# Windowed attention and a two-layer feed-forward: the weights' conversion is untied from the blocks before it, and its low words, loads and row bounds go to other engines

## The chip, the cores and the metric

The kernel runs on one core of a Trainium2 chip. The metric is the device time of one execution in microseconds. Before the change three runs took 990.71, 990.72 and 995.53 us, median 990.72. The engines are TensorE (PE, matmuls and transposes into PSUM), VectorE (DVE), ScalarE (ACT), GpSimd (POOL) and SyncE (SP, which here only starts DMAs). Each takes its instructions in the order in which the program was scheduled.

## The reference

```
scores = q k^T / 8 - slope_h |i - j|,   only 0 <= i - j < 128, else -1e9     # 8 x 8 heads, 576 rows, 64 wide
attn   = softmax(scores);   x = attn v, heads side by side: 4608 x 512
h = x @ w_in                                                               # 512 -> 2048
g = h where h >= 1;  0 where h <= -1;  (h + 1)^2 / 4 between
out = g @ w_out                                                            # 2048 -> 512, 4608 x 512
```

Q, K and V come as 32-bit floats, the weights w_in and w_out as 64-bit floats, which the kernel sees as two 32-bit words a number: a low word and a high word.

## The kernel before, in words

The 4608 rows are worked in 12 chunks of 384. For each chunk come the attention of four pairs of heads (a pair fills the 128 partitions) and then the feed-forward in 16 blocks of 128 hidden units. The program interleaves by hand: the list `segments` holds the steps of attention, the list `ffn` those of the feed-forward, and while the feed-forward of chunk c is emitted, the segments of chunk c + 1 are emitted between its steps (L799 to L807). The marks `ready` say up to which segment a chunk's attention must have been emitted before its feed-forward begins. A scheduler then orders the instructions of each engine by the order of emission and by when it expects an operand to be there; `behind(instructions, f)` (L238) adds edges, so that what f emits stands on its engine behind the given instruction of the same engine.

Attention of a pair: `scores` (L433, matmuls at L443), `soften` (L465: a VectorE operation L482 with bias and row extreme, ScalarE's exponential L484, then L490 to L495 on VectorE), `weights_t` (L499: transposes L504, ScalarE's copy L508, and two selects on GpSimd, L509 and L511, that make the tile `lu`), `values` (L525, matmuls at L538). `reach_of_v` (L380) takes the row maxima of V on VectorE (L385).

A block of the feed-forward: `layer1` (L587: 12 matmuls L590 to L592 of 16-bit high and low parts; then u by ScalarE at L597 and g by VectorE at L598 and L599), and two blocks later `layer2` (L610; in chunk 0 32-bit matmuls at L619, later 16-bit ones at L622 to L624). From chunk 1 on GpSimd makes the low part of g (L607).

The weights are converted once, while attention and feed-forward of chunk 0 run. For each of the 16 blocks:

- `fetch_weights` (L171) starts two DMAs from ScalarE's queue (L173, L175) into one of three buffers of raw words.
- `unfold` (L177): ScalarE maps the high words (L180) and the low words (L181), 128 x 1024 each, in place.
- `float32_of` (L183, VectorE at L185) joins both into a 32-bit float, once for w_in (`f_i`) and once for w_out (`wf`).
- `convert_in` (L189) also takes the row maxima of `f_i` on VectorE (L194); `convert_out` (L216) takes the row sums of |wf| on ScalarE (L219).
- `scale_in` (L197, through `scale_of` at L154): a matmul spreads the row bounds over the partitions (L152), VectorE reduces them (L159) and makes a power of two and its inverse (L161 to L163).
- `split_in` (L204): one more small product (`fall_in`, L202), the 16-bit high part on ScalarE (L210) and the low part on VectorE (L211).

Blocks 0 to 2 are converted during the attention of chunk 0: `convert_early` (L766) puts the two halves of each behind the heads listed in `EARLY` (L761). The others are converted by `convert_after(f)` (L749), emitted after layer 1 of block f for block f + 3, and each step is tied by `behind(done_g[f], ...)` to u and g of that block.

## Time and profile before

| what | value |
|---|---|
| median of three runs | 990.72 us |
| the profiled execution, its own time | 991.8 us |
| its span, first to last instruction | 989.7 us |
| mean granted TensorE clock | 0.989 |
| VectorE busy in the span | 731.6 us (74%) |
| ScalarE busy in the span | 607.2 us (61%) |
| GpSimd busy in the span | 340.6 us (34%) |

The page and the answers of the trace give times in microseconds from the first instruction of the span, and the mean time of one instruction of a group in nanoseconds. A row names the line of the kernel, the engine, the operation, the written and read tiles and their shape. "x16" is a count. The text in brackets, or behind the second bar of a group, is idle time of the engine just before the instruction and what ended it. "ACTq" and "SPq" are the DMA issues of these engines' queues; they are not counted as busy.

### The profile page before, as it was taken

The numbers are of one execution on the slowest core, as the hardware profiler recorded it, in microseconds if no ns is written. First come the engines' busy times: TensorE is split into PE (matmuls) and PEld (weight loads), VectorE is DVE, ScalarE is ACT, GpSimd is POOL, SyncE is SP. The second block draws the span as 40 slices with busy tenths as digits, with TensorE's granted clock in tenths as the row PEclk, the third lists the DMA queues.
The fourth block names the chain that finished last, engine by engine and source line by source line (L and its number), as shares of the span: only waits on it lengthen the run. The fifth ranks groups of instructions, "written<-read, shape, count | busy, mean of one in ns | idle before, by whom it ended". The sixth has DMA issues, their size and how long they took to land.

```text
span 989.7 us, 17764 instructions
## 1 busy us (share of the span) xinstructions
PE 955.0 (96%) x6181; PEld 522.2 (53%) x6181; DVE 731.6 (74%) x2089; ACT 607.2 (61%) x1509; POOL 340.6 (34%) x446
## 2 busy tenths in 40 slices
PE   8798899998999999999999999999999999999997
PEld 5444344554555555555555555555555555555553
DVE  6899798896787787687787788677677886765332
ACT  6788777666656666565665665666666655644322
POOL 5311003333334432532533533433443443334221
PEclk9799999998999999999999999999999999999999
DMA  8476441012021011112111101111201000000000
GB/s 274 134 245 201 154 141 39 12 49 72 30 59 58 25 41 63 38 30 60 62 33 52 58 25 54 63 30 50 72 30 30 33 1 1 33 2 1 33 1 32
DMA packets 53290, 59.86 MB, mean 60 GB/s; under 512 B 3408, under 2 KB 42576, under 8 KB 53200
## 3 DMA queue, kind: packets, MB, share of 16 engines
q1 hardware_dynamic: 42304, 41.82, 13.7%
q10 hardware_dynamic: 10896, 16.91, 4.9%
q8 instruction: 48, 0.79, 0.3%
q14 instruction: 42, 0.34, 0.1%
HBM read 49.28 MB, written 9.44 MB: 59 GB/s over the span
## 4 chain that ended last, share of the span: by engine, by line
PE 85%; DVE 7%; ACT 4%; DMA 1%; issue 1%; POOL 1%; ACTq 0%; SPq 0%; POOLq 0%; DVEq 0%
PE h L590 12%; PE h L592 12%; PE h L591 12%; PE acc L622 12%; PE acc L623 12%; PE acc L624 12%; PE s L459 5%; PE x L561 4%; PE p L504 3%; ACT z L484 1%; PE acc L619 1%; DMA vn<-in_v_dram 1%; DVE g L598 1%; ACT raw L181 1%; DVE g L599 1%
## 5 line engine op out<-in xcount | busy, mean ns | idle before, releaser
L607 POOL TENSOR_TENSOR gl<-g,gh 128x384 f16<-128x384 f32 x176 | 167.2, 950 | 453.5 <-ACT gh L606 442.7
L598 DVE SCALAR_TENSOR_TENSOR g<-u,half 128x384 f32<-128x384 f32 x176 | 123.9, 705 | 157.1 <-ACT u L597 144.1
L606 ACT CAST gh<-g 128x384 f16<-128x384 f32 x176 | 89.6, 509 | 189.2 <-DVE g L599 102.1
L622 PE MATMUL acc<-wo,gh 128*128 128x512 f16 x528 | 200.3, 379 | 0.0
L623 PE MATMUL acc<-wo,gh 128*128 128x512 f16 x528 | 200.2, 379 | 0.0
L624 PE MATMUL acc<-wo,gl 128*128 128x512 f16 x528 | 196.0, 379 | 0.0
L597 ACT ACTIVATE u<-h,shift,fall 128x384 f32<-128x384 f32 x176 | 116.4, 663 | 98.9 <-PE h L592 98.9
L484 ACT ACTIVATE z<-z,nmax 128x256 f32<-128x256 f32 (+2 forms) x288 | 137.7, 480 | 33.1 <-DVE nmax L482 31.1
L590 PE MATMUL h<-x,wi 128*128 128x384 f16 x384 | 125.8, 329 | 4.6 <-ACT x L570 2.8
L590 PE MATMUL h<-xh,wi 128*128 128x384 f16 x384 | 125.2, 327 | 4.3 <-ACT wi L210 2.9
L592 PE MATMUL h<-xh,wi 128*128 128x384 f16 x384 | 125.3, 326 | 1.1 <-DVE wi L211 1.1
L592 PE MATMUL h<-x,wi 128*128 128x384 f16 x384 | 126.1, 328 | 0.0
L591 PE MATMUL h<-x,wi 128*128 128x384 f16 x384 | 126.0, 328 | 0.0
L591 PE MATMUL h<-xl,wi 128*128 128x384 f16 x384 | 125.4, 327 | 0.0
L482 DVE CUSTOM_DVE_ANT_0 z<-s,near,z_of 128x256 f32<-128x256 f32 (+2 forms) x240 | 98.6, 459 | 33.7 <-PE s L459 33.5
L599 DVE SCALAR_TENSOR_TENSOR g<-h,gain,g 128x384 f32<-128x384 f32 x176 | 108.1, 615 | 3.9
L590 PEld LDWEIGHTS <-wi 128*128 128x128 f16 x768 | 75.2, 98 | 67.1 <-issue 7.5
L591 PEld LDWEIGHTS <-wi 128*128 128x128 f16 x768 | 75.4, 98 | 59.1 <-issue 7.2
L592 PEld LDWEIGHTS <-wi 128*128 128x128 f16 x768 | 75.3, 98 | 53.9 <-issue 3.6
L519 POOL TENSOR_SCALAR_AFFINE_SELECT lu<-lu 128x768 f16<-128x768 f16 x80 | 70.4, 894 | 58.2 <-DVE lu L517 57.7
L624 PEld LDWEIGHTS <-gl 128*128 128x128 f16 x528 | 51.5, 98 | 59.0 <-issue 0.4
L622 PEld LDWEIGHTS <-gh 128*128 128x128 f16 x528 | 51.6, 98 | 51.0 <-issue 1.1
(148 smaller groups left out, 1445.7 us busy)
## 6 DMA issues: line engine op xcount, KB each, us to landing
out_dram<-o SPq DMA_DIRECT2D x35, 256.0 KB, 2.1
raw<-in_moe_w_in_dram ACTq DMA_DIRECT2D x16, 512.0 KB, 4.6
raw<-in_moe_w_out_dram ACTq DMA_DIRECT2D x16, 512.0 KB, 5.5
vn<-in_v_dram SPq DMA_DIRECT2D x32, 256.0 KB, 2.8
qk<-in_q_dram SPq DMA_DIRECT2D x40, 192.0 KB, 2.4
qk<-in_k_dram SPq DMA_DIRECT2D x28, 256.0 KB, 2.8
vn<-in_v_dram SPq DMA_DIRECT2D x16, 192.0 KB, 2.6
qk<-in_k_dram SPq DMA_DIRECT2D x12, 192.0 KB, 2.5
```

The lines of the kernel that those rows point to most:

```text
L482: a = V.tensor_tensor_reduce(out=z[:, i, c0:], in0=pt[:, n, c0:], in1=r[:, c0:], op0=ALU.add, op1=ALU.min, scale=factor, scalar=3.0e38, ac ...
L484: b = S.activation(z[:, i, c0:], z[:, i, c0:], AF.Exp, bias=nmax[:, i:i + 1], scale=-1.0, accum_out=sm[:, i, 0:1])
L590: T.matmul(ph, wi[fc][:, 0, cc, :], xh, start=(cc == 0), stop=False)
L591: T.matmul(ph, wi[fc][:, 0, cc, :], xl, start=False, stop=False)
L592: T.matmul(ph, wi[fc][:, 1, cc, :], xh, start=False, stop=(cc == NCC - 1))
L597: first = S.activation(u, ph, AF.Relu, bias=shift[c] if c else quarter, scale=fall[c][:, col])
L598: V.scalar_tensor_tensor(g, u, half[c] if c else 0.5, u, ALU.min, ALU.mult)
L599: last = V.scalar_tensor_tensor(g, ph, gain[c][:, col] if c else fall[c][:, col], g, ALU.mult, ALU.max)
L607: G.tensor_tensor(gl, g, gh, ALU.subtract)
L622: T.matmul(a, gh[:, ts], wo[fc][:, 0], start=first, stop=False)
L623: T.matmul(a, gh[:, ts], wo[fc][:, 1], start=False, stop=False)
L624: T.matmul(a, gl[:, ts], wo[fc][:, 0], start=False, stop=last)
```

## The change

Seven edits, in the order of the diff:

1. The loads of the weights are started by SyncE; those of blocks 1 and 2 follow a small memset on GpSimd. That of block 0 is put behind the first two pairs' loads of Q and K.
2. The low words are mapped by GpSimd.
3. The row bounds of w_in are sums of absolute values by ScalarE instead of maxima by VectorE. Blocks 0 and 1 keep a column each; from block 2 on two blocks share a tile of two columns.
4. `scale_in` works on all columns of such a tile at once, so it is called for every second block; `fall_in` moves into it.
5. Around pair 4 (the first of chunk 1), the values of pairs 2 and 3 and the transposes of pair 3 are emitted ahead of the scores of pair 4, and the mark `ready` with them.
6. The maxima of V of pairs 4 to 7 are all emitted in step 4 instead of steps 3 and 4.
7. The ties to `done_g` go from `convert_after` and from `split_in`; `EARLY` is one head earlier in its last two entries.

```diff
     def fetch_weights(fc):
         w = raw[fc] = rawp.tile([P, 2, DM, 2], I32, name=f"raw{fc}", tag=f"raw{fc % 3}")
-        S.dma_start(w[:, 0].rearrange("p (c f) w -> p c f w", c=NCC),
-                    wi32[:, 2 * fc * P:2 * (fc + 1) * P].rearrange("(c p) (f w) -> p c f w", p=P, w=2))
-        S.dma_start(w[:, 1], wo32[fc * P:(fc + 1) * P, :].rearrange("p (f w) -> p f w", w=2))
+        if 0 < fc < 3:
+            G.memset(w[:1, :, 0, :1], 0)
+        DMA.dma_start(w[:, 0].rearrange("p (c f) w -> p c f w", c=NCC),
+                      wi32[:, 2 * fc * P:2 * (fc + 1) * P].rearrange("(c p) (f w) -> p c f w", p=P, w=2))
+        DMA.dma_start(w[:, 1], wo32[fc * P:(fc + 1) * P, :].rearrange("p (f w) -> p f w", w=2))
...
-        S.activation(low, low.bitcast(U32), AF.Copy, scale=0.9375 * 2.0 ** -29)
+        G.tensor_scalar(low, low.bitcast(U32), 0.9375 * 2.0 ** -29, None, ALU.mult)
...
         float32_of(fc, 0, f)
-        rows = column(f"rows_i{fc}", "rows")
-        V.tensor_reduce(rows, f, X, ALU.max, apply_absolute_value=True)
-        spread(f"i{fc}", rows)
+        if fc < 2 or fc % 2 == 0:
+            width = 1 if fc < 2 else 2
+            rows_i[fc] = column(f"rows_i{fc}_{width}", f"rows{width}", n=width)
+        S.activation(junk, f, AF.Abs, accum_out=rows_i[fc] if fc < 2 else rows_i[fc - fc % 2][:, fc % 2:fc % 2 + 1])
 
     def scale_in(fc):
-        s1, i1 = s_in[:, fc:fc + 1], i_in[:, fc:fc + 1]
-        scale_of(f"i{fc}", s1, i1)
+        rows = rows_i.pop(fc)
+        n = rows.shape[1]
+        s1, i1 = s_in[:, fc:fc + n], i_in[:, fc:fc + n]
+        b = bank(f"m_i{fc}")[:, :n * P]
+        across(b, rows)
+        top = column(f"top_i{fc}", f"top{n}", n=n)
+        V.tensor_reduce(top, b.rearrange("p (a w) -> p a w", w=P), X, ALU.max)
+        ti = top.bitcast(I32)
+        V.tensor_scalar(ti, ti, 0x7F800000, None, ALU.bitwise_and)
+        V.tensor_scalar(i1, top, 2.0 ** -100, 1.0 / TOP, ALU.max, ALU.mult)
+        V.reciprocal(s1, i1)
+        if fc > 1:
+            fall_in(fc, n)
...
     for p in range(p8):
+        if p == NPAIR:
+            segments.append([lambda p=p: values(p - 2)])
+            turn(2 * p - 2)
+            turn(2 * p - 1)
+            segments.append([lambda p=p: values(p - 1)])
+            ready.append(len(segments))
         segments += [[lambda p=p: scores(p, (0, 1))], [lambda p=p: scores(p, (2,))]]
...
-            segments += [[lambda d=d, x=x: behind(done_t[d], lambda: reach_of(x))] for x in {3: (4, 5), 4: (6, 7), 6: (8,), 7: (9,)}.get(p, ())]
+            segments += [[lambda d=d, x=x: behind(done_t[d], lambda: reach_of(x))] for x in {4: (4, 5, 6, 7), 6: (8,), 7: (9,)}.get(p, ())]
...
         if c == 0 and fc + 2 < NFC:
-            ops.append(lambda fc=fc: behind(done_g[fc], lambda: split_in(fc + 2)))
+            ops.append(lambda fc=fc: split_in(fc + 2))
...
             if fc + 2 < NFC:
-                behind(done_g[f], lambda: fetch_weights(fc + 2))
-            behind(done_g[f], lambda: convert_in(fc))
-            behind(done_g[f - 1 if f else f], lambda: convert_out(fc))
-        if f + 2 < NFC:
-            behind(done_g[f], lambda: scale_in(f + 2))
+                fetch_weights(fc + 2)
+            convert_in(fc)
+            convert_out(fc)
+        if f + 2 < NFC and f % 2 == 0:
+            scale_in(f + 2)
...
-    EARLY = (2, 3, 4, 5, 7, 8)
+    EARLY = (2, 3, 4, 5, 6, 7)
...
     load_first(1)
+    fetch_weights(0)
     load_v(0)
...
-    landed = S.copy(loaded, pair[0]["qr"][:, :1])
-    behind([landed.ins], lambda: fetch_weights(0))
```

More of the change, by code (lines that the diff above doesn't have):

```diff
@@ L180, in unfold @@
         S.activation(high.bitcast(F32), high.bitcast(F32), AF.Prelu, scale=2.0 ** -112, alpha=2.0 ** 32)
-        S.activation(low, low.bitcast(U32), AF.Copy, scale=0.9375 * 2.0 ** -29)
+        G.tensor_scalar(low, low.bitcast(U32), 0.9375 * 2.0 ** -29, None, ALU.mult)
     def float32_of(fc, a, out):
         V.scalar_tensor_tensor(out.bitcast(I32), raw[fc][:, a, :, 1], 3, raw[fc][:, a, :, 0], ALU.logical_shift_left, ALU.bitwise_or)
-    wide = {}
+    wide, rows_i = {}, {}
     def convert_in(fc):
@@ L192, in convert_in, with fall_in @@
         float32_of(fc, 0, f)
-        rows = column(f"rows_i{fc}", "rows")
-        V.tensor_reduce(rows, f, X, ALU.max, apply_absolute_value=True)
-        spread(f"i{fc}", rows)
+        if fc < 2 or fc % 2 == 0:
+            width = 1 if fc < 2 else 2
+            rows_i[fc] = column(f"rows_i{fc}_{width}", f"rows{width}", n=width)
+        S.activation(junk, f, AF.Abs, accum_out=rows_i[fc] if fc < 2 else rows_i[fc - fc % 2][:, fc % 2:fc % 2 + 1])
     def scale_in(fc):
-        s1, i1 = s_in[:, fc:fc + 1], i_in[:, fc:fc + 1]
-        scale_of(f"i{fc}", s1, i1)
-    def fall_in(fc):
-        V.tensor_scalar(fall[0][:, fc:fc + 1], i_in[:, fc:fc + 1], i_x[0], 0.25, ALU.mult, ALU.mult)
+        rows = rows_i.pop(fc)
[11 more added lines that the diff above has]
+            fall_in(fc, n)
+    def fall_in(fc, n=1):
+        V.tensor_scalar(fall[0][:, fc:fc + n], i_in[:, fc:fc + n], i_x[0], 0.25, ALU.mult, ALU.mult)
     def split_in(fc):
-        if fc > 1:
-            fall_in(fc)
         f, s1 = wide.pop(fc), s_in[:, fc:fc + 1]
@@ L662, in windowed_attention_then_ffn @@
             segments.append([lambda: scale_x(1)])
-        if 2 <= p <= NPAIR:
+        if 2 <= p < NPAIR:
             segments.append([lambda p=p: values(p - 2)])
-        if 1 <= p <= NPAIR:
+        if 1 <= p < NPAIR:
             turn(2 * p - 2)
@@ L668, in windowed_attention_then_ffn @@
         if p >= NPAIR:
-            segments.append([lambda p=p: values(p - 1)])
-            if p == NPAIR:
-                ready.append(len(segments))
+            if p > NPAIR:
+                segments.append([lambda p=p: values(p - 1)])
             turn(2 * p)
```

## The prediction

> **What bounds the kernel now.** I read the page first, then a table of the busy times by stage, then what stopped TensorE inside the slow stages.
>
> ```profile
> PE 955.0 (96%) x6181; PEld 522.2 (53%) x6181; DVE 731.6 (74%) x2089; ACT 607.2 (61%) x1509; POOL 340.6 (34%) x446
> ```
> ```profile
> 20.00:44.00 24.00, 16.16 (x77) 8.87 (x78) 22.91 (x82) 20.09 (x51) 8.18 (x17) 0.79 0.61 194
> 44.00:160.00 116.00, 103.39 (x497) 52.31 (x496) 100.39 (x312) 92.76 (x193) 11.04 (x31) 0.99 0.50 167
> ...
> 225.00:245.00 20.00, 15.56 (x109) 8.25 (x108) 12.85 (x39) 12.34 (x32) 9.10 (x11) 0.83 0.23 76
> 245.00:989.00 744.00, 736.49 (x4953) 403.77 (x4951) 524.85 (x1454) 428.51 (x1090) 275.98 (x323) 1.00 0.12 37
> ```
>
> The columns after the length are busy PE, PEld, DVE, ACT, POOL, then the granted TensorE clock. The kernel is bound by TensorE, but not everywhere: from 245 us on it idles 7.5 of 744 us, while it idles 7.8 of the 24 us from 20 to 44 (attention of row chunk 0) and 12.6 of the 116 us from 44 to 160 (feed-forward of chunk 0, with the conversion of the weights). VectorE is busy 22.91 of 24 there, then 100.39 of 116. So the first 160 us are bound by VectorE's queue, and the change, which works only there, can win at most those 20.4 us and some slow clock. The last rows of the argument are the waits of TensorE and VectorE themselves:
>
> ```profile
> 24.70 0.52 PE L504 MATMUL p<-ident,ep 128*128 128x128 f32 x3 [2.51 <-DVE rc L491]
> 40.27 1.11 PE L538 MATMUL x<-lu,vn 128*64 128x256 f32 x2 [2.85 <-POOL lu L511]
> 69.12 2.84 PE L619 MATMUL acc<-wf,g 128*128 128x512 f32 x6
> 110.48 4.17 PE L619 MATMUL acc<-wf,g 128*128 128x512 f32 x6 [3.07 <-DVE g L599]
> ```
> ```profile
> 22.50 0.69 DVE L385 TENSOR_REDUCE rows<-vn 128x1 f32<-128x512 f32 x1 [0.73 <-DMA vn<-in_v_dram]
> 23.34 0.69 DVE L385 TENSOR_REDUCE rows<-vn 128x1 f32<-128x512 f32 x1
> ```
> ```profile
> DVE g L598 <- ACT u L597: 6.7, 2, 3.7
> ```
>
> The bracket is the idle time before a row and who ended it. TensorE's 2.51 us at 24.70 end with a softmax step that stands behind two reductions of V (L385) on VectorE, the first of which had waited 0.73 us for its load. The 3.07 us before 110.48 end with VectorE's g.
>
> **The change part by part.** *VectorE loses work.* Sixteen maxima of the rows (L194) go, and the powers of blocks 2 to 15 come in seven pairs. This view has all of VectorE's groups between 17 and 157 us that the sum needs (busy us, mean ns):
>
> ```profile
> L211 DVE SCALAR_TENSOR_TENSOR wi<-f_i,s_in,wi 128x512 f16<-128x512 f32 x16 | 12.2, 763 | 1.7 <-ACT wi L210 1.7
> L185 DVE SCALAR_TENSOR_TENSOR wf<-raw 128x512 int32<-128x512 int32 x16 | 11.6, 723 | 0.0
> L185 DVE SCALAR_TENSOR_TENSOR f_i<-raw 128x512 int32<-128x512 int32 x16 | 11.0, 688 | 2.2 <-ACT raw L181 2.2
> L194 DVE TENSOR_REDUCE rows_i<-f_i 128x1 f32<-128x512 f32 x16 | 10.8, 678 | 0.0
> ...
> L598 DVE SCALAR_TENSOR_TENSOR g<-u 128x384 f32<-128x384 f32 x16 | 8.8, 551 | 6.9 <-ACT u L597 6.7
> L495 DVE TENSOR_TENSOR ep<-z,rc 128x384 f32<-128x384 f32 x14 | 7.9, 589 | 0.0
> L494 DVE TENSOR_TENSOR z<-z 128x384 f32<-128x384 f32 (+1 forms) x14 | 7.6, 546 | 0.0
> ...
> L159 DVE TENSOR_REDUCE top_i<-m_i 128x1 f32<-128x128 f32 x16 | 4.5, 282 | 0.2 <-PE m_i L152 0.2
> ...
> L202 DVE TENSOR_SCALAR fall<-i_in,i_x 128x1 f32<-128x1 f32 x16 | 3.1, 194 | 0.0
> ...
> L163 DVE RECIPROCAL s_in<-i_in 128x1 f32<-128x1 f32 x16 | 2.5, 157 | 0.3
> ...
> L162 DVE TENSOR_SCALAR i_in<-top_i 128x1 f32<-128x1 f32 x16 | 2.4, 149 | 0.2
> L161 DVE TENSOR_SCALAR top_i<-top_i 128x1 int32<-128x1 int32 x16 | 2.4, 148 | 0.1
> ...
> L344 DVE TENSOR_REDUCE i<-m 128x2 f32<-128x256 f32 x1 | 0.4, 414 | 0.0
> ```
> ```profile
> 27.10 0.67 DVE L194 TENSOR_REDUCE rows_i<-f_i 128x1 f32<-128x512 f32 x1
> 27.69 0.27 DVE L482 CUSTOM_DVE_ANT_0 z<-s,rel 128x128 f32<-128x128 f32 x1
> ```
>
> From start to start an L194 takes 0.59 us, its tail of 0.09 lies under the next one: 16 x 0.59 = 9.4 us. A pair saves the four small ones, 0.148 + 0.149 + 0.157 + 0.194 = 0.65, and a reduction of one column for the longer one of two (L344 has that shape), 2 x 0.282 - 0.414 = 0.15; 0.80 less five tails of 0.09 is 0.35, and seven times that 2.4 us. Together -11.8 us.
>
> *ScalarE* loses 16 low words (L181) and gains 16 sums of the form of L219.
>
> ```profile
> 27.22 1.14 ACT L181 ACTIVATE raw<-raw 128x1024 int32<-128x1024 uint32 x1
> 28.25 0.62 ACT L219 ACTIVATE junk<-wf 128x512 bf16<-128x512 f32 x1
> 28.77 0.20 ACT L219 ACTIVATION_READ_ACCUMULATOR junk<-wf 128x1 f32 x1
> 28.86 0.47 ACT L544 COPY xn<-x 128x384 f32<-128x384 f32 x1
> ```
>
> That is 16 x (0.61 - 1.03) = -6.7 us. ScalarE is not the fuller queue (92.76 of 116), so this counts nothing in the sum; it is the cover under which the u of a block comes no later. Its 32 DMA issues go too, also counted at nothing, because its busy rows run on beside them.
>
> *GpSimd gains 16 low words of 128x1024.* No such instruction is in the trace. From below, its selects move 384 columns in 0.52 us, 1.4 us for 1024. From above, its own TENSOR_SCALAR:
>
> ```profile
> L127 POOL TENSOR_SCALAR rel<-rel x6: 847/847/1092, 4.4 to 9.0; 128x256 f32<-128x256 f32 x6
> ```
> ```profile
> L511 POOL TENSOR_SCALAR_AFFINE_SELECT lu<-lu 128x384 f32<-128x384 f32 x14 | 8.6, 611 | 0.8
> L509 POOL TENSOR_SCALAR_AFFINE_SELECT lu<-lu 128x384 f32<-128x384 f32 x14 | 8.5, 612 | 52.6 <-ACT lu L508 52.6
> ```
>
> Four times 847 ns is 3.4 us, four times 1092 is 4.4. I take 3.4, the same operation: 54 us, 0.39 of the 140 us. GpSimd had 17.1 us of selects there, so it has room. The Trainium skill ("GPSIMD Engine Reference", section 7) gives about 1.9 cycles an element where the step is at most 8 bytes, as here: at its 1.2 GHz that is, as an estimate, 1.6 us. L127, with a step of 4 bytes, took 4.0 cycles an element, and the measurement decides; with the page's figure the two costs below would be halved and the sum about 4 us better.
>
> *What GpSimd's work costs VectorE.* An operation with two inputs in SBUF is slower beside GpSimd:
>
> ```profile
> L598 DVE SCALAR_TENSOR_TENSOR g<-u,half 128x384 f32<-128x384 f32 x176 | 123.9, 705 | 157.1 <-ACT u L597 144.1
> ```
> ```profile
> 28.66 0.41 DVE L494 TENSOR_TENSOR z<-z 128x256 f32<-128x256 f32 x1
> 32.06 0.66 DVE L494 TENSOR_TENSOR z<-z 128x256 f32<-128x256 f32 x1
> ```
> ```profile
> 31.73 0.72 POOL L511 TENSOR_SCALAR_AFFINE_SELECT lu<-lu 128x384 f32<-128x384 f32 x1
> ```
>
> L598 takes 551 ns in chunk 0, where GpSimd is mostly idle, and 705 later, beside gl: 1.28 times. L494 beside a select took 0.66 instead of 0.41: 1.6 times. The two-input groups above (L211, L185 twice, L598, L495, L494) sum to 59.1 us; 0.39 of them meets a low word. That is +6.4 us at 1.28, +13.8 at 1.6, and nothing from below, if they fall beside other work. I take 1.28, which is a mean over 176, not one case.
>
> *The order around pair 4.* The maxima of V of pairs 4 and 5 leave the place at 22.5: the waits of 0.73 and 0.15 there (0.9 us) go; the reductions themselves are only moved. Chunk 0's last values now come ahead of the scores of pair 4, so that pair 4's softmax fills the 3.7 us in which VectorE waited for the first u; TensorE keeps those scores for the time of the selects. -4.6 us together; from below 0.9, if the fill fails. What is late next is the selects of head 7: block 2 is converted one head earlier (EARLY 6 instead of 7), and its low word can stand on GpSimd between the selects of heads 6 and 7.
>
> *The clock.* The six L619 at 110.48 took 4.17 us instead of 2.84 after the 3.07 us gap. With 0.6 us less of L194 per block ahead of that g, and the reductions of V elsewhere, I count the gap as shortened enough for this to go: -1.4.
>
> *Waits that come.* The selects stand in GpSimd's queue, and the values matmul stands behind them. A select that comes at random finds a low word in 0.39 of the cases and waits half of 3.4: 0.66 us, 14 heads, 9.3 us. TensorE's own waits for them so far (us in total, times, longest):
>
> ```profile
> PE x L538 <- POOL lu L511: 4.1, 3, 2.9
> ```
>
> It waited three times, for seven pairs, and a pair stands behind the later of its two heads: 3/7 x 9.3 / 2 = +2.0. From above: 3.4 for each of seven pairs, 23.8.
>
> *The loads* now stand in SP's queue, in order with those of Q, K and V:
>
> ```profile
> 25.29 7.59 SPq L377 DMA_DIRECT2D vn<-in_v_dram  x2
> ```
>
> Two loads of V held that queue 7.6 us until their small memset on GpSimd had run. Weights behind such a pair are late by as much, but are fetched two blocks, some 14 us, ahead (116 us for 16 blocks is 7 a block): 0, and up to one such wait (7.6) if that lead is gone. The two new memsets hold loads 1 and 2 behind the selects of a head, in the attention of chunk 0, long before their blocks multiply: 0 as well. *The ties taken out* let the scheduler put conversions ahead of u and g. I count them at 0; they bring or cost what the rivals say.
>
> **The sum.** -11.8 + 6.4 - 4.6 - 1.4 + 2.0 = -9.4 us. The profiled run took 991.8 (span 989.7 and 2.1 around it), so 982.4; the median of the runs shown, 990.72, lies 1.1 below the profiled one, so 981.3.
>
> **The rivals.** *Nothing gained:* the overlap costs VectorE 1.6 times, 13.8 us, and the order around pair 4 brings only the 0.9. -11.8 + 13.8 - 0.9 - 1.4 + 2.0 = +1.7, which gives 992.4. For it: VectorE is the full queue, and every conversion puts its low word beside its own two-input steps. Against: 176 rows of L598 say 1.28. The Trainium skill (same page, section 1) names contention with VectorE instructions of two SBUF inputs; the trace agrees, 705 against 551 ns. That the ties bind nothing, since three buffers of raw words set the order anyway, leads to no new case: the sum counts them at 0.
>
> *Slower:* GpSimd becomes the wait. In order, a low word of 3.4 us ahead of a pair's last select delays its values matmul by that much, and TensorE, also in order, stands. The gain without the +2.0 is 11.4 us, so it decides from four pairs of seven on (13.6); five give 17.0 - 11.4 = +5.6, 996.3, all seven +12.4, 1003.1. For it: TensorE already waited 2.85 us for L511 with GpSimd nearly empty. Against: 61% of GpSimd's time is still free of low words, and the scheduler has other blocks to put between.
>
> *More gained:* the conversions run ahead into gaps, and the overlap costs nothing on the path: -11.8 - 4.6 - 1.4 = -17.8, 972.9. For it: 20.4 us of idle TensorE are there to fill. Against: ScalarE and VectorE have little slack in which to run ahead.
>
> **How the numbers follow.** The forecast (976 to 987) has 0.48, more gained (968 to 976) 0.14, nothing gained (987 to 995) 0.20, slower 0.18. The range 970 to 998 leaves out the lower half of "more" and the upper half of "slower", about 0.16. A measurement can tell about 0.5%, 5 us (two runs shown agree to 0.01 us, the third is 4.8 off): faster is below 985.8. Of the forecast some 0.41 of its 0.48 lies there; with 0.14 that is 0.55. Same: 0.07 + 0.20 = 0.27. Slower 0.18. The forecast's own range is 976 to 987.
>
> **What would show it.** Right: no L194; low words on GpSimd of about 3.4 us; L385 of pairs 4 and 5 later than the first h; TensorE's idle time from 20 to 160 us down from 20.4 to about 12; L185 and L211 some 10% longer (0.39 of 1.28); the span after 245 us unchanged. Wrong: low words near 1.5 us (more gained), or L185 waiting for GpSimd instead of ScalarE, or TensorE's waits for lu above 10 us (slower).

## The result, and the profile after

The changed kernel is slower. Five runs of it took 998.07 to 1000.71 us, median 999.65; five of the kernel before, on the same chip, 990.71 to 995.53, median 992.63. The ratio is 1.0067, with a 95% interval of 1.0050 to 1.0084, so about 6.7 us more where 9.4 less was forecast. The profiled execution took 999.68 us, its span is 997.7, its mean granted clock 0.982 (before 991.8, 989.7 and 0.989). The head of the page, after:

```profile
PE 956.7 (96%) x6181; PEld 523.3 (52%) x6181; DVE 726.5 (73%) x2038; ACT 602.8 (60%) x1524; POOL 390.6 (39%) x464
```

VectorE has 5.1 us less to do than before, ScalarE 4.4 less, GpSimd 50 more. None of these sums tells why the kernel is slower. Lines of the changed kernel stand a little lower than those of before: the low word is L183, the join L187 (was L185), the sum of w_in L198, the low part of w_in L223 (L211), the maxima of V L397 (L385), softmax's last step L507 (L495), its transposes L516 (L504), the selects L521 and L523 (L509, L511), the values L550 (L538), layer 1 L602 to L604 (L590 to L592).

The table by stage cuts the early part at 70 us. First before, then after (busy PE, PEld, DVE, ACT, POOL, then the clock):

```profile
20.00:70.00 50.00, 39.98 (x196) 21.68 (x197) 44.46 (x147) 41.95 (x93) 13.33 (x32) 0.90 0.58 187
70.00:160.00 90.00, 79.57 (x377) 39.50 (x376) 78.84 (x247) 70.89 (x150) 5.89 (x16) 0.98 0.49 162
160.00:990.00 830.00, 817.06 (x5497) 447.65 (x5495) 595.31 (x1636) 483.63 (x1227) 310.62 (x359) 1.00 0.12 37
```
```profile
20.00:70.00 50.00, 24.87 (x117) 13.20 (x115) 39.59 (x105) 36.96 (x86) 37.29 (x27) 0.71 0.61 204
70.00:160.00 90.00, 86.31 (x404) 43.90 (x403) 69.82 (x207) 59.40 (x140) 30.00 (x37) 0.97 0.45 147
160.00:998.00 838.00, 827.90 (x5558) 453.26 (x5556) 604.35 (x1669) 495.93 (x1260) 312.72 (x360) 1.00 0.12 37
```

TensorE's idle time in each stretch is its length less its busy time (the last one ends with the span, at 989.7 and 997.7). From 20 to 70 us it went from 10.0 to 25.1, from 70 to 160 from 10.4 down to 3.7, after 160 from 12.6 to 9.8. So TensorE idles 6.7 us less from 70 to 160 us, in the feed-forward of chunk 0, and 15.1 us more in the attention of chunk 0 and the first steps after it. The stretches are cut by the clock, not by the work: the last second-layer matmuls of chunk 0 start at 152.65 us before and at 166.34 after. Beside that, TensorE's busy time rose by 1.7, and its idle time before 20 us by 0.8: 15.1 - 6.7 - 2.8 + 1.7 + 0.8 = 8.1, the span's 8.0. In the same 140 us VectorE is busy 109.4 instead of 123.3, but 9.0 of these 13.9 us only come later: after 160 us it is busy 604.35 instead of 595.31.

The longest waits of TensorE there are these five (timeline of after; start, length, and in brackets the idle time before and who ended it):

```profile
38.01 0.29 PE L152 MATMUL m_i<-ident,rows_i 128*128 128x128 bf16 x1 [4.25 <-ACT junk L198]
41.32 1.12 PE L550 MATMUL x<-lu,vn 128*64 128x256 f32 x2 [2.38 <-POOL lu L523]
45.84 0.29 PE L152 MATMUL m_i<-ident,rows_i 128*128 128x128 bf16 x1 [3.40 <-ACT junk L198]
49.81 2.39 PE L550 MATMUL x<-lu,vn 128*64 128x256 f32 x10 [1.25 <-POOL lu L523]
67.80 1.54 PE L516 MATMUL p<-ident,ep 128*128 128x128 f32 x6 [6.93 <-DVE ep L507]
```

To see why the values stood so late, GpSimd's timeline at that place:

```profile
36.69 2.89 POOL L183 TENSOR_SCALAR raw<-raw 128x1024 int32<-128x1024 uint32 x1 [4.25 <-DMA raw<-in_moe_w_out_dram]
39.64 1.04 POOL L521 TENSOR_SCALAR_AFFINE_SELECT lu<-lu 128x384 f32<-128x384 f32 x1
40.75 0.52 POOL L523 TENSOR_SCALAR_AFFINE_SELECT lu<-lu 128x384 f32<-128x384 f32 x1
41.35 2.89 POOL L183 TENSOR_SCALAR raw<-raw 128x1024 int32<-128x1024 uint32 x1
44.32 1.04 POOL L521 TENSOR_SCALAR_AFFINE_SELECT lu<-lu 128x384 f32<-128x384 f32 x1
45.44 3.21 POOL L183 TENSOR_SCALAR raw<-raw 128x1024 int32<-128x1024 uint32 x1
48.72 1.04 POOL L523 TENSOR_SCALAR_AFFINE_SELECT lu<-lu 128x384 f32<-128x384 f32 x1
```

Head 6's and head 7's selects stand behind three low words, one of them between head 7's own two selects. The first low word itself stood 4.25 us for its load, and everything behind it stood too: ScalarE's copy for head 6, which its selects need, was done by 33.34 (first row below). The last select ends at 49.76. TensorE's two waits for m_i come from conversions as well. The matmul that spreads a block's row bound stands in TensorE's queue ahead of the attention still to do, and the bound is late; ScalarE and VectorE, after:

```profile
32.88 0.46 ACT L520 COPY lu<-p 128x384 f32<-128x384 f32 x1
...
36.24 1.10 ACT L182 ACTIVATE raw<-raw 128x1024 f32<-128x1024 f32 x1 [1.37 <-DMA raw<-in_moe_w_out_dram]
37.25 0.61 ACT L198 ACTIVATE junk<-f_i 128x512 bf16<-128x512 f32 x1
...
45.07 0.63 ACT L198 ACTIVATE junk<-f_i 128x512 bf16<-128x512 f32 x1 [2.64 <-DVE f_i L187]
```
```profile
44.28 0.69 DVE L187 SCALAR_TENSOR_TENSOR f_i<-raw 128x512 int32<-128x512 int32 x1 [1.07 <-POOL raw L183]
```

The sum at 37.25 stood behind a high word (L182) that waited for a load as well, so the first of the two waits comes from a load and not from a low word; the sum at 45.07 stood behind a join that waited for the low word of 41.35. At 67.80 TensorE's queue holds the transposes of pair 4 ahead of the next block's first layer. They wait for VectorE, whose rows there are:

```profile
62.20 2.45 DVE L397 TENSOR_REDUCE rows<-vn 128x1 f32<-128x512 f32 x4
64.57 0.22 DVE L503 RECIPROCAL rc<-rc 128x3 f32<-128x3 f32 x2
64.72 0.99 DVE L610 SCALAR_TENSOR_TENSOR g<-u 128x384 f32<-128x384 f32 x2
65.63 1.58 DVE L187 SCALAR_TENSOR_TENSOR wf<-raw 128x512 int32<-128x512 int32 x1
67.14 0.14 DVE L400 TENSOR_REDUCE rows<-rows 128x1 f32<-128x4 f32 x1
67.20 1.01 DVE L507 TENSOR_TENSOR ep<-z,rc 128x384 f32<-128x384 f32 x2
```

The four maxima of V of pairs 4 to 7, 2.45 us (edit 6 brought two of them here), and a join of 1.58 stand ahead of pair 4's last softmax step.

### The profile page after: what moved, and what is told of

It is laid out like the page before. It is cut to its first block, busy times and chain, and to the rows that moved or that the text cites. A ratio compares the mean times of both kernels' runs of the same rounds, so it can differ in the third digit from the quotient of the medians.

```text
span 997.7 us, 17790 instructions
## 1 busy us (share of the span) xinstructions
PE 956.7 (96%) x6181; PEld 523.3 (52%) x6181; DVE 726.5 (73%) x2038; ACT 602.8 (60%) x1524; POOL 390.6 (39%) x464
## 4 chain that ended last, share of the span: by engine, by line
PE 87%; DVE 4%; DMA 3%; POOL 2%; ACT 2%; issue 1%; SPq 0%; POOLq 0%; ACTq 0%; DVEq 0%
PE h L602 12%; PE h L604 12%; PE h L603 12%; PE acc L634 12%; PE acc L635 11%; PE acc L636 11%; PE s L471 5%; PE x L573 4%; DMA raw<-in_moe_w_out_dram 3%; PE p L516 3%; PE acc L631 2%; POOL raw L183 1%; PE s L455 1%; DMA qk<-in_q_dram 1%; ACT z L496 1%
## 5 line engine op out<-in xcount | busy, mean ns | idle before, releaser
L602 PE MATMUL h<-xh,wi 128*128 128x384 f16 x384 | 125.6, 329 | 3.4 <-DVE g L611 2.3
L602 PE MATMUL h<-x,wi 128*128 128x384 f16 x384 | 125.2, 327 | 3.0 <-DVE g L611 2.7
L604 PE MATMUL h<-x,wi 128*128 128x384 f16 x384 | 125.3, 326 | 0.0
L604 PE MATMUL h<-xh,wi 128*128 128x384 f16 x384 | 125.3, 328 | 0.0
L602 PEld LDWEIGHTS <-wi 128*128 128x128 f16 x768 | 75.2, 98 | 64.0 <-issue 7.9
L604 PEld LDWEIGHTS <-wi 128*128 128x128 f16 x768 | 75.3, 98 | 55.1 <-issue 6.7
```

The lines of the kernel that those rows point to most:

```text
L602: T.matmul(ph, wi[fc][:, 0, cc, :], xh, start=(cc == 0), stop=False)
L604: T.matmul(ph, wi[fc][:, 1, cc, :], xh, start=False, stop=(cc == NCC - 1))
```

## The experiments

Three theories at the start. *Line:* low words, each of them 3 us, stand on GpSimd ahead of the selects of heads 6 and 7, and that is the loss. *Ties:* conversions that run ahead on ScalarE and VectorE are the loss. *Order:* the scores of pair 4, now behind the values of pair 3, leave TensorE without work while it waits, and its clock falls. Each run below stands beside runs of the kernel before on its own chip, median 992.4 to 993.3 us, so a thousandth of a ratio is 1 us. In brackets stands the 95% interval. The diffs show the lines that tell an edit; `...` stands for lines left out.

### The line of GpSimd

**Conversions of blocks 2 to 4 held behind head 7**, all else as after:

```diff
-            convert_in(fc)
-            convert_out(fc)
+            behind(done_t[7] if fc < 5 else [], lambda: (convert_in(fc), convert_out(fc)))
...
-    EARLY = (2, 3, 4, 5, 6, 7)
+    EARLY = (2, 3, 4, 5, 7, 7)
```

> The changed kernel with one thing more: the conversions of blocks 2, 3 and 4 stand behind the selects of head 7 on GpSimd (and behind head 7's steps on the other engines); the low words stay on GpSimd and the ties stay out. Line: head 7's selects end before 43 us, 984 to 992 us. Ties: later blocks still run ahead, 996 to 1000. Order: 996 to 1000.

990.62 us, ratio 0.9974 (0.9958 to 0.9989), 9 us below the kernel after. GpSimd's timeline has the low words behind the last select, which now ends at 37.19 instead of 49.76:

```profile
35.92 0.68 POOL L521 TENSOR_SCALAR_AFFINE_SELECT lu<-lu 128x384 f32<-128x384 f32 x1 [0.64 <-ACT lu L520]
36.67 0.52 POOL L523 TENSOR_SCALAR_AFFINE_SELECT lu<-lu 128x384 f32<-128x384 f32 x1
37.27 9.47 POOL L183 TENSOR_SCALAR raw<-raw 128x1024 int32<-128x1024 uint32 x3
```

The time lies in the range of the line theory and outside those of the other two, and more than the whole loss against before is gone. `done_t[7]` holds instructions of VectorE, ScalarE and GpSimd, though, so the conversions stand behind head 7 on all three engines.

**The ties of edit 7 put back**, EARLY as after:

```diff
-            ops.append(lambda fc=fc: split_in(fc + 2))
+            ops.append(lambda fc=fc: behind(done_g[fc], lambda: split_in(fc + 2)))
...
-                fetch_weights(fc + 2)
-            convert_in(fc)
-            convert_out(fc)
+                behind(done_g[f], lambda: fetch_weights(fc + 2))
+            behind(done_g[f], lambda: convert_in(fc))
+            behind(done_g[f - 1 if f else f], lambda: convert_out(fc))
...
-            scale_in(f + 2)
+            behind(done_g[f], lambda: scale_in(f + 2))
```

> The changed kernel with the ties of the conversion to u and g put back (edit 7 without EARLY). Three theories. Line: on GpSimd the low words of blocks 2 to 4 stand among the selects of heads 6 and 7, so that these end at 49.8 us instead of 41.6; the ties name only instructions of ScalarE and VectorE, so they never bound the low words on GpSimd and putting them back frees nothing there: 995 to 1003 us. Ties: the conversions that ran ahead on ScalarE and VectorE are the cost: 982 to 990. Order: the scores of pair 4, now behind the values of pair 3, leave TensorE without work while it waits, and the clock falls to half: 996 to 1002.

998.79 us, ratio 1.0063 (1.0042 to 1.0083): no better than after. The ties are edges on ScalarE and VectorE, whose instructions `done_g` holds, and hold nothing on GpSimd: two low words, at 34.63 and 40.11, still stand ahead of the last selects there.

```profile
40.11 2.87 POOL L183 TENSOR_SCALAR raw<-raw 128x1024 int32<-128x1024 uint32 x1
43.05 1.04 POOL L523 TENSOR_SCALAR_AFFINE_SELECT lu<-lu 128x384 f32<-128x384 f32 x1
```

The theory of the ties had 982 to 990 and fails as the cause by itself. The last select does end earlier, at 44.09, and from 20 to 70 us TensorE idles 15.7 us instead of after's 25.1; but from 70 to 160 it idles 9.8 instead of 3.7, and the kernel is no faster. It has edits 3 and 4 beside the ties, a company that costs the kernel before 12.8 us (below); that this eats up the earlier start is argued, not shown.

**Low words back on ScalarE**, all else as after:

```diff
-        G.tensor_scalar(low, low.bitcast(U32), 0.9375 * 2.0 ** -29, None, ALU.mult)
+        S.activation(low, low.bitcast(U32), AF.Copy, scale=0.9375 * 2.0 ** -29)
```

> The changed kernel with the low words back on ScalarE, all else as changed. Line: nothing stands among the selects, head 7's end before 42 us, 982 to 991 us. Ties: conversions run ahead on ScalarE with 1 us more each, as slow as the changed kernel or slower, 998 to 1006. Order: TensorE still has no scores in the gap, but the gap is short: 993 to 999.

993.85 us, ratio 1.0006 (0.9992 to 1.0020): 6 us below after, but above the 982 to 991 of the line theory. TensorE still waits for head 7's last select:

```profile
42.39 2.40 PE L550 MATMUL x<-lu,vn 128*64 128x256 f32 x10 [5.76 <-POOL lu L523]
```

Here ScalarE is late: from 35.48 to 39.68 us it maps the high and low words of two blocks, and its copy for head 7 comes behind them, at 40.69.

**Low words back on ScalarE and the conversions held** (both edits):

```diff
-        G.tensor_scalar(low, low.bitcast(U32), 0.9375 * 2.0 ** -29, None, ALU.mult)
+        S.activation(low, low.bitcast(U32), AF.Copy, scale=0.9375 * 2.0 ** -29)
...
-            convert_in(fc)
-            convert_out(fc)
+            behind(done_t[7] if fc < 5 else [], lambda: (convert_in(fc), convert_out(fc)))
...
-    EARLY = (2, 3, 4, 5, 6, 7)
+    EARLY = (2, 3, 4, 5, 7, 7)
```

> The changed kernel with blocks 2 to 4 behind head 7 and the low words back on ScalarE, so that none of GpSimd's costs is left. If the prediction's gains were sized rightly, -11.8 - 4.6 - 1.4 = -17.8 and 973 to 978 us. If they were not, and only GpSimd's queue was harmful, as fast as the changed kernel with the same hold, 987 to 993. If ScalarE's longer conversions take its place, 993 to 998.

994.21 us, ratio 1.0023 (1.0010 to 1.0036). None of GpSimd's costs is left here, and the prediction's gains are not there either: they would have given 973 to 978. With low words on ScalarE holding gains nothing (1.7 us slower, with overlapping intervals), with low words on GpSimd it gains 9.3. What holding mends is there only with the low words on GpSimd. How much of it TensorE feels through the selects, through the row bounds or through the load, these runs don't part.

**The kernel before with low words on GpSimd**:

```diff
-        S.activation(low, low.bitcast(U32), AF.Copy, scale=0.9375 * 2.0 ** -29)
+        G.tensor_scalar(low, low.bitcast(U32), 0.9375 * 2.0 ** -29, None, ALU.mult)
```

> The kernel before with only the low words moved to GpSimd. Line: the low word of block 3 stands ahead of head 6's selects although the ties are in place, since they do not name GpSimd; values of pair 3 some 5 us late, 993 to 999 us. Ties and order: as before, 988 to 993.

994.11 us, ratio 1.0018 (1.0002 to 1.0034). This is in the range of the line theory (993 to 999). Here, with EARLY one head later and the other edits absent, only one low word stands ahead of the last two heads; it ends at 37.20, and the next select waits for ScalarE's copy until 40.85. Edit 2 costs 1.8 us instead of 6.

### The VectorE term

**The kernel before with edits 3 and 4**, ties in place:

```diff
-        V.tensor_reduce(rows, f, X, ALU.max, apply_absolute_value=True)
+        S.activation(junk, f, AF.Abs, accum_out=rows_i[fc] if fc < 2 else rows_i[fc - fc % 2][:, fc % 2:fc % 2 + 1])
...
-        if f + 2 < NFC:
+        if f + 2 < NFC and f % 2 == 0:
             behind(done_g[f], lambda: scale_in(f + 2))
```

> The kernel before with only the row bounds as ScalarE's sums and the powers in pairs (edits 3 and 4), ties kept. The prediction's term was -11.8 us of VectorE, all of it on the path: 979 to 984 us. Rival: the two queues take turns, and 16 sums of 0.61 us on ScalarE take back most of it, 988 to 994. Second rival: the pairs make a scale wait for the next block's conversion, 995 to 1000.

1005.34 us, ratio 1.0129 (1.0114 to 1.0144). This is the term of -11.8 by itself, and it came out at +12.8, beyond even the slowest of the three ranges. Stage and TensorE's waits from 60 us on:

```profile
44.00:160.00 116.00, 94.64 (x443) 47.04 (x440) 84.61 (x244) 95.47 (x204) 10.61 (x29) 0.99 0.48 160
```
```profile
PE acc L629 <- DVE g L609: 6.7, 9, 1.5
PE h L600 <- DVE g L609: 4.8, 1, 4.8
PE h L600 <- ACT wi L220: 3.3, 4, 1.5
```

VectorE is busy 84.61 us instead of 100.39 (718.8 instead of 731.6 in the whole span), so its work did go; but TensorE is busy 8.8 us less as well. From 60 us on it waits for g 11.5 us in these rows, where the kernel before has 3.9; its wait for the high parts of the weights (3.3 us) is about what it was (2.9). Two new theories: *queue*, ScalarE's sums stand ahead of u; *pair*, the power of an even block waits for the conversion of the odd one, which comes a step later.

**The sums alone** (edit 3, single powers):

```diff
-        V.tensor_reduce(rows, f, X, ALU.max, apply_absolute_value=True)
+        S.activation(junk, f, AF.Abs, accum_out=rows)
```

> The kernel before with one line changed: the row bounds of w_in are sums by ScalarE (edit 3) instead of maxima by VectorE; powers stay single (edit 4 left out), ties stay. Edits 3 and 4 together took 12.5 us more than the kernel before. Theory queue (ScalarE is the queue that u stands in, so 16 sums of 0.61 us, 9.8 us, stand ahead of a u): ratio about 1.008 to 1.011, and TensorE's waits for u and h grow as they did with both edits. Theory pair (only the scale that waits for a second block costs): about 0.992 to 0.998, since VectorE loses 9.4 us and ScalarE had 23 of 116 us idle.

989.84 us, ratio 0.9972 (0.9961 to 0.9983).

**The pairs alone** (edit 4, maxima by VectorE):

```diff
-        V.tensor_reduce(rows, f, X, ALU.max, apply_absolute_value=True)
+        V.tensor_reduce(rows_i[fc] if fc < 2 else rows_i[fc - fc % 2][:, fc % 2:fc % 2 + 1], f, X, ALU.max, apply_absolute_value=True)
...
-        if f + 2 < NFC:
+        if f + 2 < NFC and f % 2 == 0:
             behind(done_g[f], lambda: scale_in(f + 2))
```

> The kernel before with the powers of two blocks at once (edit 4) while the row bounds stay maxima by VectorE; ties stay. Theory queue: the pairs save VectorE 2.4 us, ratio 0.997 to 1.000. Theory pair: the scale of an even block stands behind the conversion of the odd one, which comes with the next step, so the first layer of every second block waits for its weights; 12.5 us and a little more, since VectorE keeps its maxima: 1.010 to 1.02, with waits of the first layer's weight loads for the 16-bit weights.

994.53 us, ratio 1.0019 (1.0006 to 1.0032). The sums alone fit the theory of the pair, the pairs alone fit neither: -2.8 and +1.9 alone, +12.8 together. The two cost in company.

**Both, and the ties taken out**:

```diff
...
-            ops.append(lambda fc=fc: behind(done_g[fc], lambda: split_in(fc + 2)))
+            ops.append(lambda fc=fc: split_in(fc + 2))
...
-                behind(done_g[f], lambda: fetch_weights(fc + 2))
-            behind(done_g[f], lambda: convert_in(fc))
-            behind(done_g[f - 1 if f else f], lambda: convert_out(fc))
-        if f + 2 < NFC:
-            behind(done_g[f], lambda: scale_in(f + 2))
+                fetch_weights(fc + 2)
+            convert_in(fc)
+            convert_out(fc)
+        if f + 2 < NFC and f % 2 == 0:
+            scale_in(f + 2)
```

> The kernel before with edits 3 and 4 (sums by ScalarE, powers of two blocks) and, unlike the run that had these two with the ties, with the ties of the conversion taken out too; EARLY, low words, loads and order as before. The sums alone took 2.8 us off, the pairs alone added 1.9, both with the ties added 12.5, and undoing both in the kernel after changed 0.9. Theory tie: the two cost only where the conversion of the next block may not run ahead, so without ties the 12.5 us go: ratio 0.996 to 1.000. Theory queue: sums and pairs together cost in any order as long as the conversion is not crowded out by something else: 1.008 to 1.013.

991.98 us, ratio 0.9989 (0.9973 to 1.0005). The stage from 44 to 160 us, to be held against the row above:

```profile
44.00:160.00 116.00, 105.13 (x511) 54.97 (x509) 92.51 (x267) 99.49 (x221) 13.25 (x33) 0.98 0.51 168
```

ScalarE is fuller than in that run, 99.49 us, and TensorE busy 10.5 us more: the 12.8 need the ties, and a full queue of ScalarE doesn't explain them. With the ties, a pair's second sum may stand on ScalarE only behind a block's u, and the pair's power only behind that sum; that this is the way by which the ties cost is argued, the run shows only that they do.

**The kernel after with edits 3 and 4 undone**:

```diff
-        S.activation(junk, f, AF.Abs, accum_out=rows_i[fc] if fc < 2 else rows_i[fc - fc % 2][:, fc % 2:fc % 2 + 1])
+        V.tensor_reduce(rows, f, X, ALU.max, apply_absolute_value=True)
...
-        if f + 2 < NFC and f % 2 == 0:
+        if f + 2 < NFC:
             scale_in(f + 2)
```

> The kernel after with edits 3 and 4 undone: maxima by VectorE, single powers; low words, loads, order and untied conversion as after. If the 12.5 us that edits 3 and 4 cost the kernel before are in the kernel after as well: ratio to before about 0.994 (987 us). If what binds the kernel after is only the line at heads 6 and 7 (holding the conversions there gave 9.0 us): 1.004 to 1.008, as after.

1000.52 us, ratio 1.0070 (1.0051 to 1.0090), against 1.0067 for after: edits 3 and 4 neither help nor cost there.

**The same with the conversions held** (this diff and that of the first experiment):

```diff
-        S.activation(junk, f, AF.Abs, accum_out=rows_i[fc] if fc < 2 else rows_i[fc - fc % 2][:, fc % 2:fc % 2 + 1])
+        V.tensor_reduce(rows, f, X, ALU.max, apply_absolute_value=True)
...
+            behind(done_t[7] if fc < 5 else [], lambda: (convert_in(fc), convert_out(fc)))
```

> The kernel after with edits 3 and 4 undone and the conversions of blocks 2 to 4 held behind head 7. Holding alone gave 990.6, ratio 0.997. If the cost of the sums and pairs and the cost of the line at heads 6 and 7 are two separate terms: 990.6 less 12.5, 978 us, ratio 0.985, faster than every kernel so far. If they are the same time seen twice: 0.994 to 0.998, no better than holding alone.

991.90 us, ratio 0.9991 (0.9981 to 1.0000), against 0.9974 with the conversions held and edits 3 and 4 in. The 978 us of two separate costs did not come. So in the untied kernel edits 3 and 4 are worth 0.3 us without the hold and 1.7 with it, neither clear of the intervals, and holding gains 7.9 us here too. Of this run and the one before it, from 20 to 70 us:

```profile
20.00:70.00 50.00, 30.40 (x129) 15.78 (x128) 43.34 (x109) 31.37 (x71) 36.19 (x27) 0.69 0.54 183
```
```profile
20.00:70.00 50.00, 37.60 (x162) 19.81 (x161) 44.66 (x119) 33.25 (x76) 37.74 (x32) 0.73 0.54 180
```

The first is without holding, the second with it: VectorE and GpSimd have nearly the same work in both, and TensorE 7.2 us more. Not how full the queues are decides, but the order in them.

The end of head 7's last select on GpSimd goes along with the time, but only roughly. The kernel before, where it ends at 41.60 us, and the runs in which it ends by 43.8 (held with low words on either engine or without edits 3 and 4, low words on ScalarE, low words on GpSimd in the kernel before) took 990.6 to 994.2; the three in which it ends at 44.09 (ties back), 45.55 (edits 3 and 4 undone) and 49.76 (after) took 998.8 to 1000.5. Within each group the order is not kept.

### The order around pair 4

**Edit 5 alone, in the kernel before**:

```diff
+        if p == NPAIR:
+            segments.append([lambda p=p: values(p - 2)])
+            turn(2 * p - 2)
+            turn(2 * p - 1)
+            segments.append([lambda p=p: values(p - 1)])
+            ready.append(len(segments))
         segments += [[lambda p=p: scores(p, (0, 1))], [lambda p=p: scores(p, (2,))]]
```

> The kernel before with only the order around pair 4 (edit 5). The prediction's term was -3.7 for the filled wait for the first u: 986 to 990 us. Rival: TensorE loses the scores of pair 4 as work to do while it waits for the selects of head 7, and the clock stays low longer, 993 to 998.

988.40 us, ratio 0.9958 (0.9941 to 0.9975): -4.2, where the prediction had 3.7 for the fill. The wait that was to be filled did go: from 17 to 157 us VectorE stands 2.9 us for u, at most 1.1 at a time, where the kernel before has 6.7 and 3.7.

**Edit 6 alone, in the kernel before**:

```diff
... (within one line)
-{3: (4, 5), 4: (6, 7), 6: (8,), 7: (9,)}
+{4: (4, 5, 6, 7), 6: (8,), 7: (9,)}
```

> The kernel before with edit 6 alone: the maxima of V of pairs 4 to 7 all in step 4. The prediction counted the two waits of 0.73 and 0.15 us as gone: 0.9 us, ratio 0.999. If the four reductions in one place hold up the softmax of chunk 1 instead, up to 4 x 0.7 us, 1.001 to 1.003.

986.85 us, ratio 0.9943 (0.9929 to 0.9957): -5.7, where 0.9 was counted, and outside both ranges. The fastest of all the kernels tried. TensorE idles 15.0 us from 20 to 160 us instead of 20.4; of the three waits that the prediction showed, 2.51 us at 24.70, 2.85 at 40.27 and 3.07 at 110.48, none is left above 1 us at its place; the longest new one is 2.14, at 36.19.

**Edits 5 and 6 together** (both diffs):

```diff
+            segments.append([lambda p=p: values(p - 1)])
+            ready.append(len(segments))
         segments += [[lambda p=p: scores(p, (0, 1))], [lambda p=p: scores(p, (2,))]]
...
-{3: (4, 5), 4: (6, 7), 6: (8,), 7: (9,)}
+{4: (4, 5, 6, 7), 6: (8,), 7: (9,)}
```

> The kernel before with edits 5 and 6 together: the order around pair 4 and the maxima of V of pairs 4 to 7 in step 4. This is the prediction's term of -4.6 us by itself. Alone the order gave -4.2 us and the maxima -5.7. If they win different idle time: ratio 0.990 (983 us). If they win the same one, 0.9935 to 0.996, as each alone.

994.66 us, ratio 1.0019 (1.0009 to 1.0029): the two gains together are a loss, which neither forecast had. VectorE with edit 6 alone, then VectorE and TensorE with both:

```profile
38.44 2.45 DVE L385 TENSOR_REDUCE rows<-vn 128x1 f32<-128x512 f32 x4
```
```profile
44.32 1.27 DVE L385 TENSOR_REDUCE rows<-vn 128x1 f32<-128x512 f32 x2
45.51 0.17 DVE L491 RECIPROCAL rc<-rc 128x3 f32<-128x3 f32 x1
45.59 1.25 DVE L385 TENSOR_REDUCE rows<-vn 128x1 f32<-128x512 f32 x2
46.75 0.17 DVE L491 RECIPROCAL rc<-rc 128x3 f32<-128x3 f32 x1
46.84 0.59 DVE L584 SCALAR_TENSOR_TENSOR xl<-xn,s_x,xh 128x384 f16<-128x384 f32 x1
```
```profile
47.48 0.48 PE L591 MATMUL h<-xl,wi 128*128 128x384 f16 x1 [2.86 <-DVE xl L584]
```

Alone, edit 6 puts the four maxima at 38.44, before the first layer of chunk 0. With the order of edit 5 they come at 44.32, after that layer has begun, directly ahead of the xl that it waits for, and TensorE stands 2.86 us. That is about half of the 6.1 us by which this run is behind edit 5 alone; the waits for the row bounds of the weights (m_i) grow too, from 1.3 to 5.1 us up to 160. In the kernel after they come at 62.20, ahead of pair 4's softmax, with the wait of 6.93 us behind them.

**Edit 5 with the conversion untied**:

```diff
+            segments.append([lambda p=p: values(p - 1)])
+            ready.append(len(segments))
...
-            ops.append(lambda fc=fc: behind(done_g[fc], lambda: split_in(fc + 2)))
+            ops.append(lambda fc=fc: split_in(fc + 2))
...
-            behind(done_g[f], lambda: convert_in(fc))
-            behind(done_g[f - 1 if f else f], lambda: convert_out(fc))
+            convert_in(fc)
+            convert_out(fc)
...
```

> The kernel before with edit 5 (order around pair 4) and without the ties of the conversion; EARLY, low words, loads, sums and pairs as before. Alone they gave -4.2 and -2.0 us. If they fill different idle time: 0.9937 (986.7 us), faster than every kernel so far. If the conversion run ahead fills the same wait for u that pair 4 fills: 0.995 to 0.997.

990.53 us, ratio 0.9985 (0.9967 to 1.0003). It fits neither range: not even what the order gives alone.

### The rest

**Untied alone, in the kernel before**, EARLY as before:

```diff
-            ops.append(lambda fc=fc: behind(done_g[fc], lambda: split_in(fc + 2)))
+            ops.append(lambda fc=fc: split_in(fc + 2))
...
-            behind(done_g[f], lambda: convert_in(fc))
-            behind(done_g[f - 1 if f else f], lambda: convert_out(fc))
+            convert_in(fc)
+            convert_out(fc)
...
```

> The kernel before with only the ties taken out of the conversion (edit 7 without EARLY). The prediction's term for this was 0: 989 to 994 us. Rival: free of ties, conversions of later blocks stand ahead of u, of softmax steps and of copies on ScalarE and VectorE, 995 to 1000. Second rival: they fill gaps, 980 to 987.

990.78 us, ratio 0.9982 (0.9970 to 0.9993), in the range of the prediction's term.

**The loads on SyncE alone (edit 1), in the kernel before**:

```diff
+        if 0 < fc < 3:
+            G.memset(w[:1, :, 0, :1], 0)
...
-        S.dma_start(w[:, 1], wo32[fc * P:(fc + 1) * P, :].rearrange("p (f w) -> p f w", w=2))
+        DMA.dma_start(w[:, 1], wo32[fc * P:(fc + 1) * P, :].rearrange("p (f w) -> p f w", w=2))
...
```

> The kernel before with edit 1 alone: loads of the weights started by SyncE, those of blocks 1 and 2 behind a small memset on GpSimd, that of block 0 behind the first two pairs' loads. After the line at heads 6 and 7 is taken out, the kernel after with held conversions is 2.3 us faster than before, where order (-4.2), untying (-2.0), low words on GpSimd (+1.3) and sums with pairs (-1.0) add up to -5.9; 3.6 us are open. Theory loads: they are here, 1.003 to 1.005, with ScalarE's high words waiting for their load. Theory of the prediction: 0.999 to 1.001.

990.87 us, ratio 0.9983 (0.9967 to 0.9999): no cost, rather a small gain. No run is the kernel after with edit 1 alone undone; the wait of 4.25 us for a load ahead of the low words there is 2.47 us with edits 3 and 4 undone and none with the ties back, and both are as slow as after.

**The kernel after with edits 2, 4 and 7 undone**, so with 1, 3, 5 and 6:

```diff
-        G.tensor_scalar(low, low.bitcast(U32), 0.9375 * 2.0 ** -29, None, ALU.mult)
+        S.activation(low, low.bitcast(U32), AF.Copy, scale=0.9375 * 2.0 ** -29)
...
-        if f + 2 < NFC and f % 2 == 0:
-            scale_in(f + 2)
+        if f + 2 < NFC:
+            behind(done_g[f], lambda: scale_in(f + 2))
```

> The kernel after with edits 2, 4 and 7 undone: low words on ScalarE, single powers, the ties in place; loads by SyncE, sums by ScalarE, order and maxima of V as after. Alone these four gave -1.7, -2.8, -4.2 and -5.7 us. If what the kernel after lost lies in edits 2, 4 and 7 alone: ratio 0.986 to 0.992 (979 to 985 us), faster than every kernel so far. If the sums on top of the low words fill ScalarE so far that it stands ahead of u: 0.996 to 1.002.

991.67 us, ratio 0.9993 (0.9983 to 1.0004). Four edits that alone gave -1.7, -2.8, -4.2 and -5.7 give 0.7 together. So not all of the loss lies in edits 2, 4 and 7. The time fits the other range, but not by its reason: VectorE stands for u only 3.0 us from 20 to 160. Edits 5 and 6 spoil each other here as well: the four maxima stand at 46.41 us, ahead of pair 4's softmax, and behind them TensorE waits:

```profile
49.90 0.90 PE L506 MATMUL p<-ident,ep 128*128 128x128 f32 x3 [4.81 <-DVE ep L497]
```

## Why the prediction was wrong

**The premise.** "The first 160 us are bound by VectorE's queue" was read from its share, 22.91 of 24 and 100.39 of 116 us. It failed. VectorE had 5.1 us less to do in the kernel after, and the span grew by 8.0. Sixteen maxima less were worth 2.8 us in the kernel before; with the pairs, 0.3 in the kernel after and 1.7 there with the conversions held. A queue that is full nine tenths of the time is not yet the one that TensorE waits for: of its own waits that the prediction quoted, one was ended by GpSimd (2.85 us) and two by VectorE (2.51 and 3.07), and VectorE itself had stood for ScalarE's u (6.7) and for a load (0.73).

**VectorE's work, -11.8.** The work went about as priced (with the slower joins 5.1 us net, -11.8 + 6.4 = -5.4 in the prediction); on the path it was worth 0.3 us (after against the run without edits 3 and 4), and with the ties +12.8. This is the step that failed most: a term of engine time was counted one for one as time of the span.

**VectorE beside GpSimd, +6.4.** The size was about right in engine time, the place wrong. These groups of after stand against those of before:

```profile
L183 POOL TENSOR_SCALAR raw<-raw 128x1024 int32<-128x1024 uint32 x16 | 49.0, 3062 | 27.2 <-DMA raw<-in_moe_w_out_dram 20.0 <-DVE g L610 3.9 <-DVE top_i L207 2.8
L187 DVE SCALAR_TENSOR_TENSOR wf<-raw 128x512 int32<-128x512 int32 x16 | 14.0, 877 | 3.0 <-POOL raw L183 3.0
L223 DVE SCALAR_TENSOR_TENSOR wi<-f_i,s_in,wi 128x512 f16<-128x512 f32 x16 | 13.8, 885 | 5.8 <-ACT wi L222 5.7
L187 DVE SCALAR_TENSOR_TENSOR f_i<-raw 128x512 int32<-128x512 int32 x16 | 11.9, 756 | 2.4 <-POOL raw L183 2.4
```

The three VectorE groups sum to 39.7 us instead of 34.8, +4.9, where 6.4 was counted for six groups. The low word took 3.06 us, 3.4 was taken. The Trainium skill ("GPSIMD Engine Reference", section 7) would have had 1.6 us by the estimate in the prediction; the measurement is nearly twice that.

**Selects behind low words, +2.0.** The step "a select that comes at random finds a low word in 0.39 of the cases" failed. Low words don't come at random: the scheduler put three ahead of the last two heads, 9.0 us, and a wait of 4.25 for a load ahead of them. The prediction had named this place (EARLY 6 instead of 7) and given it no price of its own. Holding those conversions is worth 9.3 us. With it failed the step that selects alone would carry the delay: TensorE's waits for lu were 3.6 us, those for the row bounds 7.7. Edit 2 as a whole cost 6.1 (after against low words on ScalarE); the prediction's two terms for it, 6.4 + 2.0, come near that by luck, with a false sharing-out.

**The order around pair 4, -4.6.** The fill was right alone (-4.2 for 3.7). "The reductions themselves are only moved" failed: where they land depends on when the first layer begins, and with edit 5 it begins before them. Alone edit 6 brought 5.7 us for the 0.9 that were counted. Together the two edits measured +1.9.

**Ties and loads, 0 each:** -1.8 and -1.7 alone, about right; in the kernel after a load did hold GpSimd's line for 4.25 us. **The clock, -1.4:** it didn't come. From 110 to 120 us the granted clock is 0.83 in both kernels; in after six second-layer matmuls at 111.57 took 4.54 us, instead of 2.84, behind gaps of only 0.64 and 1.54. From 20 to 70 us the clock fell from 0.90 to 0.71, the mean from 0.989 to 0.982.

The sum with measured terms: edit 2 +6.1, edits 3 and 4 -0.3 (both taken out of after), edits 5 and 6 +1.9, ties -1.8, loads -1.7 (put into before) is +4.2, of the 6.7 found. What is left, 2.5, is about what five terms with intervals of 1 to 2 us each leave open, and the terms are not independent, as edits 5 and 6 show; it was not settled. The change of EARLY has no run of its own.

**The rivals.** "Slower: GpSimd becomes the wait" gave the right side and its mechanism, a low word ahead of a pair's last select. Its price was for five to seven pairs of seven. In fact few pairs were hit, but by several low words in a row, and TensorE waited longer for the row bounds (m_i, 4.25 and 3.40 us at 38.01 and 45.84), which the prediction didn't name, than for the selects.

**What was to be seen:** no L194, low words of about 3 us, the maxima of pairs 4 and 5 later than the first h, a join some 10% or more slower, all came. TensorE's idle time from 20 to 160 us rose from 20.4 to 28.8 instead of falling to 12; after 245 us it is 8.2 before and 9.5 after. Of the signs set for "slower" one came, the join did wait for GpSimd (5.4 us in the two rows above), and one did not: TensorE's waits for lu were 3.6 us, not above 10.

## What to carry to other kernels

Price a change of an in-order schedule by what will stand directly ahead of the operation that the bound engine waits for, not by how many microseconds leave a busy engine: two kernels with nearly the same work in each queue from 20 to 70 us differed by 8 us. When long steps move to a quiet engine, look for the few short steps there that the bound engine waits for, and hold the long ones behind the last of them on that engine; an edge on another engine's instructions doesn't. And edits that gain alone (-4.2, -5.7) can lose together (+1.9), so measure them in the company in which they will stand; edit 6 alone was the best kernel here, 0.9943 (0.9929 to 0.9957).

## What the runs showed of the hardware

Beside a low word, not only VectorE's operations of two inputs were long. In after this small step with one input takes 0.16 us by itself and 1.08 within a low word on GpSimd:

```profile
85.26 0.16 DVE L209 TENSOR_SCALAR top_i<-top_i 128x2 int32<-128x2 int32 x1
95.15 1.08 DVE L209 TENSOR_SCALAR top_i<-top_i 128x2 int32<-128x2 int32 x1
```
```profile
94.90 3.15 POOL L183 TENSOR_SCALAR raw<-raw 128x1024 int32<-128x1024 uint32 x1 [2.77 <-DVE top_i L207]
```

And the slowing of a join is not spread evenly: 24 of the 32 L187 of after take at most 0.71 us, about as before, and eight take 0.92 to 1.58 (one of them at 65.63 above). Standing within a low word does not always cost either: the L223 at 42.46 took 0.75 us within the low word of 41.35 to 44.24. The slower mean comes from a few long ones.
